# Attention and gated MLP on one core: key loads by another queue, values earlier, and the last convolutions in PSUM

## The chip, the cores and the metric

The kernel runs on one core of a Trainium2 chip. The metric is device time in microseconds; the median of the runs counts. The engines are TensorE (PE in the profile), VectorE (DVE), ScalarE (ACT), GpSimd (POOL) and SyncE (SP), which issues DMAs here. Each works through its own queue of instructions in program order; semaphores tie the queues together. The 16 DMA engines are shared by every queue that issues DMAs.

## What is computed

Four batches of 12288 queries of width 128 attend to 768 keys, which come from pooling a 384 x 32 map by 4 x 4 and a projection; the keys are also the values. The result goes through a gated projection with a causal convolution of five taps per channel.

```python
kv_pool = kv.reshape(B, H // r, r, W // r, r, C).mean(axis=(2, 4))
k = v = kv_pool.reshape(B, -1, C) @ w_sr
s = (q @ k.transpose(0, 2, 1)) / sqrt(C)
a = exp(s - s.max(-1)); a /= a.sum(-1) + 1e-9
x = a @ v
gate = sigmoid(sum(conv_w[t] * x[n + t - 4] for t in range(5)))
out = (gate * (x @ w_val)) @ w_out
```

Arrays arrive with channels first, so that the channel is the partition; the weights of the gated part arrive as 64-bit floats in one array `w_moe` and are converted on the chip.

## The kernel before

**Tiling.** A batch is 24 groups of 512 queries, a group four tiles of 128. There are 96 groups and 384 tiles in one pipeline; the order of every engine's work is written out by hand (`manual_schedule`). `t` counts tiles, `gi` and `mj` are the group and tile (0 to 3) one tile behind, and `k` is the group's place in its batch (0 to 23).

**One tile.** TensorE computes scores (`score`, L314) in three passes over a high and a low part of queries and keys, into one of three pairs of PSUM banks `s`. DVE takes the row maximum (L320), ScalarE the Exp with its sum (L325), DVE the reciprocal (L332, L334), ScalarE the high half-precision part of the probabilities (`p_hi`, L343) and DVE the low part (`p_lo`, L347). After two tiles, SyncE issues one transpose by DMA of both parts (L352) into `pt`.

**One group.** Two groups later TensorE multiplies `pt` with the values (`av_slice`, L361), in 18 products spread over four tiles; the last six need the last third of the values, high and low (`vh`, `vl`). ScalarE writes the result to `x` (L376). Convolution (GpSimd, `conv_step`, L390 and L395), tanh (L439), the two products (L443, L453), DVE's product (`g_h`, L448), eviction (L463) and store (L467) follow over the next five groups. Queries are loaded for two groups at once, in even groups (L281), and stored in even groups too.

**Preparing the next batch.** While a batch runs, the keys of the next one are made. `load_kv` (L114) loads two of 16 pieces (768 KB) into one of three buffers `kvt`, issued by SyncE in the second tile of groups 0, 1, 3, 6, 8, 10, 13 and 15. DVE sums a third of a piece per slot (`pool_kv`, L119); slots are the first three tiles of each group, counted as `3 * k + j`, and `BLOCK`, `THIRDS` and `slots` say which slot sums what: 14 slots for a quarter of the keys, of which 12 sum, one holds `column_max` (L169) and one `keys_low` (GpSimd, L212 and L214). TensorE projects a quarter at groups 7, 12, 16 and 21 (L201), ScalarE writes `vt` (L202) and the high keys (L206). A scale per column (L190 to L194, a diagonal by GpSimd at L182) follows in group 22. The values are then made in thirds: products with the diagonal (L221), a copy by ScalarE (L223), the high part (`values_high`, L226) and the low part (`values_low`, L229) on GpSimd. The first third is made in group 23, the others in groups 0 and 1 of the batch itself; the low parts come in the third tile of groups 0, 1 and 2.

**Start.** The first batch's 16 pieces are loaded by SyncE (L494), with the first queries, `w_sr`, the second half of the first query pair (`load_second`), `w_moe` and the second query pair. GpSimd adds rows of pieces 3, 6, 9 and 12 in advance (`presum`, L130), DVE sums the rest (L119), then the keys are projected and split (L142 to L155), and the pipeline begins. `trickle` holds small work that is done one item a tile, among it the conversion of `w_moe` and five diagonal matrices `dw` for a convolution on TensorE (`conv_pe`) that nothing calls.

**End.** Behind the loop stand the last seven groups, n7 to n1, from L633. GpSimd convolves n3 (`conv_pool`, L429 and L433), DVE n4, n2 and n1 (`conv_dve`, L419 and L421), n1 in two halves, with an accumulator `fast` in SBUF. `two()` takes a pair of PSUM banks, `misc()` a single one.

Of the kernel before, what the change touches and what calls it, by code (L numbers as in the profile page):

```python
# [27 lines left out]
def attn_moe_kernel(ctx, tc, qT, kvT, w_sr, w_moe, outT):  # L28
# [37 lines left out]
    dw = const.tile([C, TAPS, C], F32, name="dw")  # L66
    wval, wout, cwt = wm[:, 0:C], wm[:, C:2 * C], wm[:, 2 * C:]

    def load_moe():

        if w_moe.dtype == F32:
            nc.sync.dma_start(out=wm, in_=w_moe)
            return []
        raw, rest, more = (work.tile([C, 2 * GQ], F32, name=n, bufs=k)
                           for n, k in (("acc", 2), ("tap0", 1), ("tap1", 1)))
        raw = raw.bitcast(I32)[:, :2 * NW]
        nc.sync.dma_start(out=raw, in_=w_moe.bitcast(I32))
        words = raw.rearrange("c (n w) -> c w n", w=2)
        lo, hi = words[:, 0], words[:, 1]
        sign, ex, a = (rest.bitcast(I32)[:, i * NW:(i + 1) * NW] for i in range(3))  # L80
        t, low = more.bitcast(I32)[:, :NW], more[:, NW:2 * NW]
        v = nc.vector

        def two(out, in_, s1, op0, s2, op1, v=nc.vector):
# [25 lines left out]

    def load_kv(b, st, i):

        t = kvp.tile([C, 2, R, PC * R], F32, name="kvt")
        nc.sync.dma_start(out=t, in_=kvT[b, i:i + 2].rearrange("n c r x -> c n r x"))  # L114
# [120 lines left out]
    BLOCK = 14  # L235
    THIRDS = [n for n in range(BLOCK) if n not in (4, 9)]
    slots = {}
    for n in range(3 * PIECES):
        q, i = divmod(n, 12)
        slots[6 + BLOCK * q + THIRDS[i]] = n  # L240
    loads = {}
    for n in range(0, 3 * PIECES, 6):
        first = next(s for s, i in slots.items() if i == n) // 3
        loads.setdefault(max(first - 3, 0), []).append(n // 3)

    def setup_product(k, st):
        for q, at_k in enumerate((7, 12, 16, 21)):
            if k == at_k:
                return project_quarter(st, q)
        if k == 23:  # L250
            return values(st, 0)

    def setup_vector(k, j, st):
# [5 lines left out]
        q, n = divmod(s - 6, BLOCK)  # L259
        if n == 4 and 1 <= q <= 3:  # L260
            column_max(st, q - 1)
        if n == 9 and 1 <= q <= 3:
            keys_low(st, q - 1)
        if (k, j) == (21, 2):
            column_max(st, 3)
            st["scale"] = column_scale(st)
        if k == 22 and j < 2:
            for _ in range(3 - j):
                st["scale"].pop(0)()
        if (k, j) == (22, 2):  # L270
            keys_low(st, 3)
            st["scale"].pop(0)()

    def load_pair(g, n, parts=1):
# [4 lines left out]
        def load(i, k):  # L279
            t0 = g.t0 + i * GQ  # L280
            nc.sync.dma_start(out=q[:, i:i + k],  # L281
# [6 lines left out]
        return lambda: load(1, 1)  # L288
# [122 lines left out]
    def conv_pe(g, m, c0, c1):  # L411
        for k in range(TAPS):
            nc.tensor.matmul(m, dw[:, k], g.x[:, k + c0:k + c1], start=(k == 0),
                             stop=(k == TAPS - 1))
        return m

    def conv_dve(g, c0=0, c1=GQ):
        s = work.tile([C, GQ], F32, name="fast")[:, :c1 - c0]
        nc.vector.tensor_scalar_mul(out=s, in0=g.x[:, c0:c1], scalar1=cwt[:, 0:1])  # L419
        for k in range(1, TAPS):  # L420
            nc.vector.scalar_tensor_tensor(out=s, in0=g.x[:, k + c0:k + c1],  # L421
                                           scalar=cwt[:, k:k + 1], in1=s,
                                           op0=ALU.mult, op1=ALU.add)
        return s
# [77 lines left out]
    load_second()  # L502
    convert = load_moe()
    load_pair(at(2), at(3))
    warm = misc()
    for i in (3, 6, 9, 12):
        presum(st, i)
    k0 = c0 = 0
    low = None
    for i in range(PIECES):  # L510
# [23 lines left out]
    score(at(0), 0, early=True)  # L534
    g_qh(at(1))
# [3 lines left out]
    trickle += [lambda k=k: nc.gpsimd.tensor_scalar(  # L539
        out=dw[:, k], in0=ident, scalar1=cwt[:, k:k + 1], scalar2=1.0, op0=ALU.mult, op1=ALU.mult)  # L540
        for k in range(TAPS)]
# [6 lines left out]
    for t in range(NT * G + LAG):  # L548
# [34 lines left out]
        if gi > 1 and k < 2 and mj == 1:  # L583
            evac = values(now, k + 1)
# [18 lines left out]
        if ahead is not None and mj == 1 and k in (8, 13, 17, 22):  # L603
            keys_high(ahead, (8, 13, 17, 22).index(k))
# [4 lines left out]
        if gi >= NG and k < 3 and mj == 2:  # L609
            values_low(now, k)  # L610
# [11 lines left out]
        if mj == 3 and k == 23 and ahead is not None:  # L622
            values_high(ahead, 0)
        if mj == 3 and gi > 1 and k < 2:
            values_high(now, k + 1)
# [22 lines left out]
    gate4 = conv_dve(n4)  # L648
# [3 lines left out]
    b0, b1 = two()  # L652
    n6.m, n5.m = g_out(n6.h, b0), g_out(n5.h, b1)
    new_x(n2)
    g_x(n2, n2.av)
    avs = [c[:, :half] for c in two()]
    new_x(n1)
    for av, c in zip(avs, (0, half)):
        j = c // P
        av_range(n1, av, 0, len(AV_ORDER), j, j + NT // 2)  # L660
        if c == 0:
# [4 lines left out]
            n4.th = g_tanh(gate4)  # L666
        g_x(n1, av, c, c + half)
    a0, a1 = two()
    n4.m, n3.m = g_val(n4, a0), g_val(n3, a1)
    halo(n2, n4, nc.vector)  # L670
    gate2 = conv_dve(n2)
    n3.th = g_tanh(gate3, work.tile([C, GQ], F32, name="th2"))
    n4.h = g_h(n4.th, n4.m)
    n3.h = g_h(n3.th, n3.m, "hh")
    b0, b1 = two()
    n2.m = g_val(n2, b0)
    n4.m = g_out(n4.h, misc())
    n3.m = g_out(n3.h, b1)
    n2.th = g_tanh(gate2)
# [4 lines left out]
    n1.th = work.tile([C, GQ], F32, name="th2")  # L684
    c0, c1 = two()
    ms = [g_val(n1, m[:, :half], c, c + half) for m, c in ((c0, 0), (c1, half))]
    gates = [conv_dve(n1, 0, half)]
    n2.h = g_h(n2.th, n2.m)
    gates.append(conv_dve(n1, half, GQ))
    for gate, c in zip(gates, (0, half)):  # L690
        g_tanh(gate, n1.th[:, c:c + half])
    out_tile(n2)
    n2.m = g_out(n2.h, misc())
    hs = [g_h(n1.th[:, c:c + half], m) for m, c in zip(ms, (0, half))]
    g_evac(n2, n2.m)
    store(n2)
    outs = two()
    for h, c, o in zip(hs, (0, half), outs):
        g_evac(n1, g_out(h, o[:, :half]), c, c + half)
# [29 lines left out]
```

## Time and profile before

| what | us |
|---|---|
| runs, lowest, median and highest | 1024.54, 1026.29, 1028.73 |
| the profiled execution | 1028.8 |
| its span, first to last instruction | 1027.0 |
| mean granted TensorE clock | 0.987 |

The profile shows one execution. Its span is shorter than its time by what lies around the instructions. Times in the profile are microseconds from the start of the span, unless marked ns. A row of a timeline gives start, duration, engine, line of the kernel, operation, output and inputs by their names in the program, shapes, a count, and in brackets how long the engine idled before and who ended that. `SPq` is SyncE issuing. In rows of groups, the numbers after the bar are busy time in all, mean duration in ns, and idle time before with what ended it.

### The profile page before, as it was taken

The numbers are of one execution on the slowest core, as the hardware profiler recorded it, in microseconds if no ns is written. First come the engines' busy times: TensorE is split into PE (matmuls) and PEld (weight loads), VectorE is DVE, ScalarE is ACT, GpSimd is POOL, SyncE is SP. The second block draws the span as 40 slices with busy tenths as digits, with TensorE's granted clock in tenths as the row PEclk, the third lists the DMA queues.
The fourth block names the chain that finished last, engine by engine and source line by source line (L and its number), as shares of the span: only waits on it lengthen the run. The fifth ranks groups of instructions, "written<-read, shape, count | busy, mean of one in ns | idle before, by whom it ended". The sixth has DMA issues, their size and how long they took to land.

```text
span 1027.0 us, 15084 instructions
## 1 busy us (share of the span) xinstructions
PE 979.7 (95%) x4549; PEld 653.6 (64%) x4549; DVE 941.1 (92%) x1864; ACT 912.8 (89%) x1584; POOL 859.5 (84%) x641
## 2 busy tenths in 40 slices
PE   3789999999999999999999998999999999999997
PEld 2656666666666656666666665666666666666663
DVE  5899999999989989999999997999998999999987
ACT  1779999999989989999999997999999999999993
POOL 3349988988997978889898987898899889989983
PEclk9899999999999999999999998999999999999998
DMA  8699999999999999999999999999999999999993
GB/s 319 126 238 220 231 230 221 247 216 218 222 248 234 233 220 231 248 231 222 226 233 238 229 247 208 219 250 214 238 209 232 210 210 209 223 211 210 210 181 111
DMA packets 619329, 227.82 MB, mean 222 GB/s; under 512 B 598129, under 2 KB 598513, under 8 KB 619249
## 3 DMA queue, kind: packets, MB, share of 16 engines
q1 hardware_dynamic: 619248, 226.86, 107.3%
q8 instruction: 37, 0.61, 0.2%
q14 instruction: 44, 0.35, 0.1%
HBM read 50.66 MB, written 25.17 MB: 74 GB/s over the span
## 4 chain that ended last, share of the span: by engine, by line
PE 81%; DVE 6%; DMA 4%; POOL 3%; ACT 2%; issue 1%; POOLq 0%; DVEq 0%; ACTq 0%
PE s L314 33%; PE av L361 32%; PE m L443 7%; PE m L453 7%; DMA pt<-hl 4%; DVE hl L347 2%; DVE nm L320 2%; POOL acc L395 1%; POOL tap L390 1%; ACT hl L343 1%; ACT s L325 1%; DVE pool L119 0%; DVE h L448 0%; PE s L453 0%; PE m L221 0%
## 5 line engine op out<-in xcount | busy, mean ns | idle before, releaser
L395 POOL TENSOR_TENSOR acc<-acc,tap 128x1024 f32<-128x1024 f32 x184 | 437.0, 2375 | 6.7
L361 PE MATMUL av<-pt,vh 128*128 128x512 f16 x1140 | 408.7, 383 | 12.9 <-DMA pt<-hl 6.7
L347 DVE SCALAR_TENSOR_TENSOR hl<-s,r,hl 128x768 f16<-128x768 f32 x384 | 388.7, 1012 | 20.3 <-ACT hl L343 16.1
L320 DVE TENSOR_REDUCE nm<-s 128x1 f32<-128x768 f32 x384 | 363.1, 945 | 27.7 <-PE s L314 24.6
L343 ACT ACTIVATE hl<-s,r 128x768 f16<-128x768 f32 x384 | 346.1, 901 | 46.8 <-DVE r L334 30.4
L325 ACT ACTIVATE s<-s,nm 128x768 f32<-128x768 f32 x384 | 335.5, 874 | 23.7 <-DVE nm L320 20.6
L314 PE MATMUL s<-kh,qh 128*128 128x384 f32 x768 | 289.3, 458 | 6.8 <-DVE z L332 5.8
L361 PEld LDWEIGHTS <-vh 128*128 128x128 f16 x1164 | 113.5, 98 | 170.1 <-issue 80.9
L361 PE MATMUL av<-pt,vl 128*128 128x512 f16 x570 | 217.1, 381 | 4.5 <-POOL vl L229 4.5
L314 PEld LDWEIGHTS s<-kh,qh 128*128 128x128 f32 x768 | 146.6, 193 | 95.2 <-issue 50.2
L390 POOL TENSOR_SCALAR tap<-x,wm 128x1024 f32<-128x1024 f32 x184 | 204.1, 1123 | 0.0
L314 PE MATMUL s<-kh,ql 128*128 128x384 f32 x768 | 197.9, 338 | 0.0
L314 PE MATMUL s<-kl,qh 128*128 128x384 f32 x768 | 197.6, 338 | 0.0
L296 POOL TENSOR_TENSOR ql<-q,qh 128x512 fp32r<-128x512 f32 x96 | 122.7, 1279 | 49.5 <-ACT qh L292 49.5
L314 PEld LDWEIGHTS s<-kl,qh 128*128 128x128 f32 x768 | 140.7, 190 | 0.0
L314 PEld LDWEIGHTS s<-kh,ql 128*128 128x128 f32 x768 | 140.5, 190 | 0.0
L361 PEld LDWEIGHTS <-vl 128*128 128x128 f16 x582 | 57.6, 99 | 59.2 <-issue 32.3
L390 POOL TENSOR_SCALAR acc<-x,wm 128x1024 f32<-128x1024 f32 x46 | 51.5, 1119 | 52.3 <-ACT x L376 52.2
L453 PE MATMUL m<-h,wm 128*128 128x512 f32 x184 | 94.0, 592 | 0.7 <-DVE h L448 0.7
L443 PE MATMUL m<-x,wm 128*128 128x512 f32 x180 | 91.9, 592 | 0.0
L334 DVE RECIPROCAL r<-z 128x1 f32<-128x1 f32 x384 | 63.0, 164 | 13.1
L325 ACT ACTIVATION_READ_ACCUMULATOR s<-s,nm 128x1 f32 x384 | 74.5, 194 | 0.0
(73 smaller groups left out, 669.3 us busy)
## 6 DMA issues: line engine op xcount, KB each, us to landing
q<-in_q SPq DMA_DIRECT2D x47, 512.0 KB, 4.6
out<-o SPq DMA_DIRECT2D x47, 512.0 KB, 3.8
kvt<-in_kv SPq DMA_DIRECT2D x24, 768.0 KB, 5.5
pt<-in_kv SPq DMA_DIRECT2D x6, 768.0 KB, 9.7
pt<-hl SPq DMA_TRANSPOSE x192, 6.5
pt<-in_kv SPq DMA_DIRECT2D x4, 384.0 KB, 7.8
q<-in_q SPq DMA_DIRECT2D x2, 256.0 KB, 11.2
acc<-in_w_moe SPq DMA_DIRECT2D x1, 261.0 KB, 10.0
```

Of the source, the lines that this page charges most:

```text
L296: nc.gpsimd.tensor_tensor(out=g.ql, in0=g.q, in1=g.qh.bitcast(F32), op=ALU.subtract)
L314: nc.tensor.matmul(s[:, h, :HALF], a[:, sl], k[:, h * HALF:(h + 1) * HALF], start=(i == 0), stop=(i == 2))
L320: nc.vector.tensor_reduce(out=nm, in_=g.s[j], axis=AX.XY, op=ALU.max, negate=True)
L325: nc.scalar.activation(out=g.s[j], in_=g.s[j], func=AF.Exp, bias=g.nm.pop(j), accum_out=g.z[j])
L334: nc.vector.reciprocal(out=g.r[j], in_=z)
L343: nc.scalar.activation(out=part(g, j, 0), in_=g.s[j], func=AF.Copy, scale=g.r[j])
L347: nc.vector.scalar_tensor_tensor(out=part(g, j, 1), in0=g.s.pop(j), scalar=g.r.pop(j), in1=part(g, j, 0), op0=ALU.mult, op1=ALU.subtract)
L361: nc.tensor.matmul(out, g.st[v][:, k * P:(k + 1) * P], g.pt[:, j0:j1, a * NCH + k], start=(i == 0), stop=(i == len(AV_ORDER) - 1))
L390: nc.gpsimd.tensor_scalar(out=t, in0=g.two[:, k:k + 2 * GQ], scalar1=cwt[:, k:k + 1], scalar2=1.0, op0=ALU.mult, op1=ALU.mult)
L395: nc.gpsimd.tensor_tensor(out=g.acc, in0=g.acc, in1=t, op=ALU.add)
L443: nc.tensor.matmul(m, wval, g.x[:, HALO + c0:HALO + c1], start=True, stop=True)
L453: nc.tensor.matmul(m, wout, h, start=True, stop=True)
```

## The change

- Key loads are issued by ScalarE's queue, at the end of the second tile's work of groups 1, 3, ... 15.
- Blocks have 13 slots and begin at slot 9 instead of 6; the low keys leave the slots for the fourth tile of groups 8, 13, 17 and 21. The last projection moves from group 21 to 20, high keys from 22 to 21, the scale from 22 to 21.
- Values are made in groups 22 and 23 of the batch before and in group 0; high and low part both follow in the fourth tile of the same group.
- At the start, the second half of the first query pair, `w_moe` and the second query pair are issued by ScalarE's queue and later; pieces 6 and 10 are presummed instead of 3, 6, 9 and 12.
- `dw`, its five products and `conv_pe` are gone.
- At the end, DVE's convolutions accumulate in PSUM (`two()` for n4 and n2, `misc()` for n1), and their order changes; the banks of the values' products are used again for the outputs.

```diff
-    dw = const.tile([C, TAPS, C], F32, name="dw")
...
-        nc.sync.dma_start(out=raw, in_=w_moe.bitcast(I32))
+        nc.scalar.dma_start(out=raw, in_=w_moe.bitcast(I32))
...
     def load_kv(b, st, i):
 
         t = kvp.tile([C, 2, R, PC * R], F32, name="kvt")
-        nc.sync.dma_start(out=t, in_=kvT[b, i:i + 2].rearrange("n c r x -> c n r x"))
+        nc.scalar.dma_start(out=t, in_=kvT[b, i:i + 2].rearrange("n c r x -> c n r x"))
...
-    BLOCK = 14
-    THIRDS = [n for n in range(BLOCK) if n not in (4, 9)]
+    BLOCK, SUMS = 13, 9
+    THIRDS = [n for n in range(BLOCK) if n != 4]
     slots = {}
     for n in range(3 * PIECES):
         q, i = divmod(n, 12)
-        slots[6 + BLOCK * q + THIRDS[i]] = n
-    loads = {}
-    for n in range(0, 3 * PIECES, 6):
-        first = next(s for s, i in slots.items() if i == n) // 3
-        loads.setdefault(max(first - 3, 0), []).append(n // 3)
+        slots[SUMS + BLOCK * q + THIRDS[i]] = n
 
     def setup_product(k, st):
-        for q, at_k in enumerate((7, 12, 16, 21)):
+        for q, at_k in enumerate((7, 12, 16, 20)):
             if k == at_k:
                 return project_quarter(st, q)
-        if k == 23:
-            return values(st, 0)
+        if k in (22, 23):
+            return values(st, k - 22)
...
-        q, n = divmod(s - 6, BLOCK)
+        q, n = divmod(s - SUMS, BLOCK)
         if n == 4 and 1 <= q <= 3:
             column_max(st, q - 1)
-        if n == 9 and 1 <= q <= 3:
-            keys_low(st, q - 1)
-        if (k, j) == (21, 2):
+        if (k, j) == (20, 2):
             column_max(st, 3)
             st["scale"] = column_scale(st)
-        if k == 22 and j < 2:
-            for _ in range(3 - j):
+        if k == 21:
+            for _ in range((3, 2, 1)[j]):
                 st["scale"].pop(0)()
-        if (k, j) == (22, 2):
-            keys_low(st, 3)
-            st["scale"].pop(0)()
...
         load(0, 1)
-        return lambda: load(1, 1)
+        return lambda: load(1, 1, nc.scalar)
...
-    def conv_dve(g, c0=0, c1=GQ):
-        s = work.tile([C, GQ], F32, name="fast")[:, :c1 - c0]
-        nc.vector.tensor_scalar_mul(out=s, in0=g.x[:, c0:c1], scalar1=cwt[:, 0:1])
+    def conv_dve(g, acc, c0=0, c1=GQ):
+        nc.vector.tensor_scalar_mul(out=acc, in0=g.x[:, c0:c1], scalar1=cwt[:, 0:1])
         for k in range(1, TAPS):
-            nc.vector.scalar_tensor_tensor(out=s, in0=g.x[:, k + c0:k + c1],
-                                           scalar=cwt[:, k:k + 1], in1=s,
+            nc.vector.scalar_tensor_tensor(out=acc, in0=g.x[:, k + c0:k + c1],
+                                           scalar=cwt[:, k:k + 1], in1=acc,
                                            op0=ALU.mult, op1=ALU.add)
-        return s
...
-    load_second()
-    convert = load_moe()
-    load_pair(at(2), at(3))
     warm = misc()
-    for i in (3, 6, 9, 12):
+    for i in (6, 10):
         presum(st, i)
...
+        if i == 13:
+            load_second()
...
     score(at(0), 0, early=True)
+    convert = load_moe()
+    load_pair(at(2), at(3), eng=nc.scalar)
...
-        if gi > 1 and k < 2 and mj == 1:
-            evac = values(now, k + 1)
+        if gi > 1 and k == 0 and mj == 1:
+            evac = values(now, 2)
...
-        if ahead is not None and mj == 1 and k in (8, 13, 17, 22):
-            keys_high(ahead, (8, 13, 17, 22).index(k))
+        if ahead is not None and mj == 1 and k in (8, 13, 17, 21):
+            keys_high(ahead, (8, 13, 17, 21).index(k))
...
-        if gi >= NG and k < 3 and mj == 2:
-            values_low(now, k)
...
-        if ahead is not None and mj == 1:
-            for i in loads.get(k, ()):
-                load_kv(b + 1, ahead, i)
+        if ahead is not None and mj == 1 and k % 2 and k < PIECES:
+            load_kv(b + 1, ahead, k - 1)
...
-        if mj == 3 and k == 23 and ahead is not None:
-            values_high(ahead, 0)
-        if mj == 3 and gi > 1 and k < 2:
-            values_high(now, k + 1)
+        if ahead is not None and mj == 3 and k in (8, 13, 17, 21):
+            keys_low(ahead, (8, 13, 17, 21).index(k))
+        if mj == 3 and (k in (22, 23) and ahead is not None or k == 0 and gi > 0):
+            for f in (values_high, values_low):
+                f(ahead if k else now, (k - 22) % NG)
...
-    gate4 = conv_dve(n4)
+    acc4, acc2 = two()
+    conv_dve(n4, acc4)
...
-    b0, b1 = two()
-    n6.m, n5.m = g_out(n6.h, b0), g_out(n5.h, b1)
+    n6.m, n5.m = g_out(n6.h, a0), g_out(n5.h, a1)
     new_x(n2)
     g_x(n2, n2.av)
+    halo(n2, n4, nc.vector)
+    conv_dve(n2, acc2)
...
+    acc1 = misc()
+    conv_dve(n1, acc1[:, :half], 0, half)
     a0, a1 = two()
     n4.m, n3.m = g_val(n4, a0), g_val(n3, a1)
-    halo(n2, n4, nc.vector)
-    gate2 = conv_dve(n2)
     n3.th = g_tanh(gate3, work.tile([C, GQ], F32, name="th2"))
     n4.h = g_h(n4.th, n4.m)
     n3.h = g_h(n3.th, n3.m, "hh")
+    conv_dve(n1, acc1[:, half:], half, GQ)
+    n2.th = g_tanh(acc2)
     b0, b1 = two()
     n2.m = g_val(n2, b0)
-    n4.m = g_out(n4.h, misc())
-    n3.m = g_out(n3.h, b1)
-    n2.th = g_tanh(gate2)
+    n4.m = g_out(n4.h, a0)
+    n3.m = g_out(n3.h, a1)
+    n1.th = work.tile([C, GQ], F32, name="th2")
+    g_tanh(acc1[:, :half], n1.th[:, :half])
+    g_tanh(acc1[:, half:], n1.th[:, half:])
+    n2.h = g_h(n2.th, n2.m)
...
-    gates = [conv_dve(n1, 0, half)]
-    n2.h = g_h(n2.th, n2.m)
-    gates.append(conv_dve(n1, half, GQ))
-    for gate, c in zip(gates, (0, half)):
-        g_tanh(gate, n1.th[:, c:c + half])
+    hs = [g_h(n1.th[:, c:c + half], m) for m, c in zip(ms, (0, half))]
     out_tile(n2)
-    n2.m = g_out(n2.h, misc())
-    hs = [g_h(n1.th[:, c:c + half], m) for m, c in zip(ms, (0, half))]
+    n2.m = g_out(n2.h, b1)
...
-    outs = two()
-    for h, c, o in zip(hs, (0, half), outs):
-        g_evac(n1, g_out(h, o[:, :half]), c, c + half)
+    for h, c, o in zip(hs, (0, half), (c0, c1)):
+        g_evac(n1, g_out(h, o[:, half:]), c, c + half)
         store(n1, c, c + half)
```

More of the change, by code (lines that the diff above doesn't have):

```diff
@@ L71, in load_moe @@
         if w_moe.dtype == F32:
-            nc.sync.dma_start(out=wm, in_=w_moe)
+            nc.scalar.dma_start(out=wm, in_=w_moe)
             return []
@@ L258, in setup_vector, with load_pair, load @@
             pool_kv(st, i, a * PC // 3, (a + 1) * PC // 3)
-        q, n = divmod(s - 6, BLOCK)
+        q, n = divmod(s - SUMS, BLOCK)
         if n == 4 and 1 <= q <= 3:
             column_max(st, q - 1)
-        if n == 9 and 1 <= q <= 3:
-            keys_low(st, q - 1)
-        if (k, j) == (21, 2):
+        if (k, j) == (20, 2):
             column_max(st, 3)
             st["scale"] = column_scale(st)
-        if k == 22 and j < 2:
-            for _ in range(3 - j):
+        if k == 21:
+            for _ in range((3, 2, 1)[j]):
                 st["scale"].pop(0)()
-        if (k, j) == (22, 2):
-            keys_low(st, 3)
-            st["scale"].pop(0)()
-    def load_pair(g, n, parts=1):
+    def load_pair(g, n, parts=1, eng=nc.sync):
         q = io.tile([C, 2, GQ], F32, name="q", bufs=3)
         g.q, n.q = q[:, 0], q[:, 1]
-        def load(i, k):
+        def load(i, k, eng=eng):
             t0 = g.t0 + i * GQ
-            nc.sync.dma_start(out=q[:, i:i + k],
+            eng.dma_start(out=q[:, i:i + k],
                               in_=qT[g.b, :, t0:t0 + k * GQ].rearrange("c (i x) -> c i x", i=k))
@@ L409, in conv_step @@
             g.gate, at(g.i + 1).gate = g.acc[:, :GQ], g.acc[:, GQ:]
[L411 to L415, printed above, removed]
-    def conv_dve(g, c0=0, c1=GQ):
-        s = work.tile([C, GQ], F32, name="fast")[:, :c1 - c0]
-        nc.vector.tensor_scalar_mul(out=s, in0=g.x[:, c0:c1], scalar1=cwt[:, 0:1])
+    def conv_dve(g, acc, c0=0, c1=GQ):
+        nc.vector.tensor_scalar_mul(out=acc, in0=g.x[:, c0:c1], scalar1=cwt[:, 0:1])
         for k in range(1, TAPS):
-            nc.vector.scalar_tensor_tensor(out=s, in0=g.x[:, k + c0:k + c1],
-                                           scalar=cwt[:, k:k + 1], in1=s,
+            nc.vector.scalar_tensor_tensor(out=acc, in0=g.x[:, k + c0:k + c1],
+                                           scalar=cwt[:, k:k + 1], in1=acc,
                                            op0=ALU.mult, op1=ALU.add)
-        return s
     def conv_pool(g):
@@ L538, in attn_moe_kernel @@
     trickle += [lambda n=n: scaling[n]() for n in range(6)] + convert
-    trickle += [lambda k=k: nc.gpsimd.tensor_scalar(
-        out=dw[:, k], in0=ident, scalar1=cwt[:, k:k + 1], scalar2=1.0, op0=ALU.mult, op1=ALU.mult)
-        for k in range(TAPS)]
     def drip():
@@ L665, in attn_moe_kernel @@
             store_pair(n5)
-            n4.th = g_tanh(gate4)
         g_x(n1, av, c, c + half)
+        if c == 0:
+            n4.th = g_tanh(acc4)
+    acc1 = misc()
+    conv_dve(n1, acc1[:, :half], 0, half)
     a0, a1 = two()
     n4.m, n3.m = g_val(n4, a0), g_val(n3, a1)
-    halo(n2, n4, nc.vector)
-    gate2 = conv_dve(n2)
     n3.th = g_tanh(gate3, work.tile([C, GQ], F32, name="th2"))
@@ L683, in attn_moe_kernel @@
     store_pair(n3)
-    n1.th = work.tile([C, GQ], F32, name="th2")
     c0, c1 = two()
     ms = [g_val(n1, m[:, :half], c, c + half) for m, c in ((c0, 0), (c1, half))]
-    gates = [conv_dve(n1, 0, half)]
-    n2.h = g_h(n2.th, n2.m)
-    gates.append(conv_dve(n1, half, GQ))
-    for gate, c in zip(gates, (0, half)):
-        g_tanh(gate, n1.th[:, c:c + half])
+    hs = [g_h(n1.th[:, c:c + half], m) for m, c in zip(ms, (0, half))]
     out_tile(n2)
-    n2.m = g_out(n2.h, misc())
-    hs = [g_h(n1.th[:, c:c + half], m) for m, c in zip(ms, (0, half))]
+    n2.m = g_out(n2.h, b1)
     g_evac(n2, n2.m)
     store(n2)
-    outs = two()
-    for h, c, o in zip(hs, (0, half), outs):
-        g_evac(n1, g_out(h, o[:, :half]), c, c + half)
+    for h, c, o in zip(hs, (0, half), (c0, c1)):
+        g_evac(n1, g_out(h, o[:, half:]), c, c + half)
         store(n1, c, c + half)
```

## The prediction

> **What bounds the kernel now.** I read the page's busy shares first, then the list of the chain that ended last, then windows of one batch each, and last SyncE's own timeline.
>
> ```profile
> PE 979.7 (95%) x4549; PEld 653.6 (64%) x4549; DVE 941.1 (92%) x1864; ACT 912.8 (89%) x1584; POOL 859.5 (84%) x641
> PE 81%; DVE 6%; DMA 4%; POOL 3%; ACT 2%; issue 1%; POOLq 0%; DVEq 0%; ACTq 0%
> 936.30 1.31 PE av L361 x6
> 946.13 1.31 PE av L361 x6
> 28.60:266.70 238.10, 225.27 (x1056) 152.22 (x1055) 228.01 (x476) 217.69 (x379) 190.76 (x149) 0.99 1.08 220
> 266.70:513.50 246.80, 241.07 (x1127) 160.79 (x1125) 230.49 (x466) 227.87 (x395) 217.59 (x160) 0.99 1.12 231
> 513.50:760.10 246.60, 241.91 (x1127) 161.33 (x1125) 230.44 (x466) 227.63 (x396) 217.55 (x160) 0.99 1.13 230
> 760.10:988.80 228.70, 227.20 (x1069) 151.68 (x1067) 208.56 (x392) 215.91 (x371) 204.76 (x145) 1.00 1.08 210
> ```
>
> The two AV rows of the chain are the same place of two neighbouring groups of the last batch: a group takes 946.13 - 936.30 = 9.83 us while TensorE never waits. The four window rows begin and end at a batch's first Exp (columns: length, busy of PE, PEld, DVE, ACT, POOL, then granted clock, DMA share, GB/s); the last covers 23 groups. At 9.83 us, 24 groups are 236.0 us. Batches 0 to 2 also prepare the next batch's keys, and TensorE's part of that is small:
>
> ```profile
> L201 PE MATMUL m<-pool,wsr 128*128 128x192 f32 x8 | 2.0, 326 | 0.0
> L221 PE MATMUL m<-diag,vt 128*128 128x128 f32 x12 | 1.9, 279 | 0.0
> ```
>
> 236.0 + 2.0 + 1.9 = 239.9 us is thus what TensorE asks of batch 1 (rows of that batch). Batch 1 is 246.8 and batch 2 is 246.6, so 6.9 + 6.7 = 13.6 us are lost in them. Where, the chain and two window rows say:
>
> ```profile
> 345.61 8.11 DMA pt<-hl
> 365.93 10.10 DMA pt<-hl
> 611.20 11.36 DMA pt<-hl
> 618.40:628.60 10.20, 7.00 (x20) 3.80 (x19) 5.39 (x13) 5.16 (x9) 7.97 (x5) 0.67 1.09 212
> 201.10:211.20 10.10, 9.61 (x45) 6.25 (x43) 9.89 (x22) 9.65 (x19) 7.58 (x6) 1.00 1.12 258
> PE av L361 <- DMA pt<-hl: 6.7, 4, 3.2
> PE av L361 <- POOL vl L229: 4.5, 3, 1.5
> 299.69 0.67 POOL L229 TENSOR_TENSOR vl<-v,vh 128x256 f16<-128x256 f32 x1
> ```
>
> TensorE waits in the AV for two things: a transpose of the probabilities that lands late (four times, and a long stop also lowers the granted clock, 0.67 at 618 us), and GpSimd's low part of the last third of the values, 1.5 us once per batch from batch 1 on. SyncE's timeline tells why the transposes are late:
>
> ```profile
> 604.78 0.54 SPq L281 DMA_DIRECT2D q<-in_q  x1
> 605.42 4.55 SPq L352 DMA_TRANSPOSE pt<-hl  x1
> 610.02 0.57 SPq L114 DMA_DIRECT2D kvt<-in_kv  x1
> 610.69 0.42 SPq L467 DMA_DIRECT2D out<-o  x1
> 611.20 8.67 SPq L352 DMA_TRANSPOSE pt<-hl  x1
> 627.74 0.54 SPq L281 DMA_DIRECT2D q<-in_q  x1
> 803.11 3.64 SPq L352 DMA_TRANSPOSE pt<-hl  x1
> L352 SPq DMA_TRANSPOSE pt<-hl x192: 3556/4547/8674, 34.7 to 999.8; - x192
> L114 SPq DMA_DIRECT2D kvt<-in_kv x24: 564/575/777, 38.4 to 685.8; - x24
> ```
>
> From one q load to the next, two groups later, SyncE needs 627.74 - 604.78 = 22.96 us here, against 2 x 9.83 = 19.66 us of TensorE. A transpose with nothing ahead takes 3.64 us to issue; the one behind a key load and a store takes 8.67. With eight key loads per batch the queue falls behind until TensorE stops. In batch 3, with no key loads, TensorE is idle for 228.7 - 227.2 = 1.5 us in all, which is the values' wait: no stop on a transpose is left. So the bound is TensorE, with SyncE's queue as second bound wherever keys are loaded.
>
> **The change part by part.**
>
> *Key loads* (24, in odd groups, ScalarE's queue). SyncE loses per load the issue of 0.575 us plus about 0.1 between instructions, 8 x 0.67 = 5.4 us per batch. The load's bytes still use the 16 DMA engines, so part of the stretch of the transposes remains; but now they stand beside transposes only, in groups with no q load or store. Per pair of groups SyncE then needs, by its median, 4 x 4.547 + 0.54 + 0.42 and six gaps of 0.1, some 19.7 us: about TensorE's pace of 19.66 to 20.0 with setup, instead of 22.96. Falling behind by a fraction of a microsecond per pair, eight times, it does not reach the limit. Of the 13.6 us I leave 0.4 per batch lost: -12.8, which includes the values' wait of 1.5 in each of the two batches. Bounds: -3.0 (only that wait goes) and -13.6; somewhat lower still if L201 and L221 overlap other matmuls.
>
> What ScalarE pays is not in this trace, since it issues no DMA. Its rows:
>
> ```profile
> L343 ACT ACTIVATE hl<-s,r 128x768 f16<-128x768 f32 x384 | 346.1, 901 | 46.8 <-DVE r L334 30.4
> 404.70 0.61 ACT L292 CAST qh<-q 128x512 fp32r<-128x512 f32 x1
> 405.30 0.90 ACT L343 ACTIVATE hl<-s,r 128x768 f16<-128x768 f32 x1
> ```
>
> The load comes behind the probabilities' high part (L343, 0.90 us). ScalarE's instructions begin before the one ahead has ended (405.30 against 404.70 + 0.61), so its sequencer works ahead, and an issue of 0.575 us fits under 0.90: I cost it at nothing. Without that cover it is 24 x 0.575 = 13.8 us at most, since the next Exp queues behind it, and DVE's z, reciprocal and low part behind that. Its wait for a free key buffer is over by then: the load of group 7 takes the buffer of group 1's load, last summed in group 5. Bounds per load 0 and 0.575 by SyncE's rows, if the issue meets no other queue (a rival below).
>
> *Values a group sooner*. TensorE's and GpSimd's instructions stay in number; the last low part moves from group 2 to group 0, two groups ahead of its use. GpSimd does it where no tap runs (fourth tile), so the 1.5 us goes: -1.5 in batch 3. *Denser sums*: 13 of 13 slots hold DVE work instead of 13 of 14, 0.2 of a 0.41 us sum per group. DVE's 230.5 of 246.8 us has room; if it hasn't, 18 groups x 0.08 = 1.5 us per batch. Taken at nothing. *Keys' low parts* (four per batch on GpSimd) move to the same fourth tile, ahead of ql, which TensorE uses three tiles later: nothing. The five unused diagonal products on GpSimd (batch 0) go; nothing waits for them. *Batch 0* has the 0.5 us of the row at 201.10: -0.5.
>
> *Start.*
>
> ```profile
> 16.92 2.06 DVE L119 TENSOR_REDUCE pool<-pt 128x48 f32<-128x192 f32 x3
> 20.51 2.07 DVE L119 TENSOR_REDUCE pool<-pt 128x48 f32<-128x192 f32 x3 [1.52 <-POOL pt L130]
> 13.91 0.35 DVE L119 TENSOR_REDUCE pool<-pt 128x48 f32<-128x192 f32 x1 [1.88 <-POOL pt L130]
> 23.39 0.94 DVE L119 TENSOR_REDUCE pool<-pt 128x48 f32<-128x768 f32 x1
> 28.67 0.88 ACT L325 ACTIVATE s<-s,nm 128x768 f32<-128x768 f32 x1 [2.25 <-DVE nm L320]
> ```
>
> Piece 12 is no longer presummed by GpSimd, for which DVE idles 1.52 us; DVE sums it whole, 0.94 (four rows summed, as at 23.39) instead of 0.35 (presummed, as at 13.91). Presums move from 9 to 10 and are the same there; piece 3's goes in a stretch where DVE waits for data. 1.52 - 0.60 = 0.9, plus a little as piece 15 loses company in the DMA: -1.0. ScalarE's two late loads (2 x 0.57 at most) precede an Exp that idles 2.25 us.
>
> *End.*
>
> ```profile
> L421 DVE SCALAR_TENSOR_TENSOR fast<-x,wm,fast 128x512 f32<-128x512 f32 x8 | 9.3, 1160 | 0.3
> L448 DVE SCALAR_TENSOR_TENSOR h<-th,s 128x512 f32<-128x512 f32 x3 | 2.1, 685 | 0.7 <-PE s L443 0.4 <-ACT th L439 0.3
> L421 DVE SCALAR_TENSOR_TENSOR fast<-x,wm,fast 128x256 f32<-128x256 f32 x8 | 3.9, 485 | 0.3
> L448 DVE SCALAR_TENSOR_TENSOR h<-th,s 128x256 f32<-128x256 f32 x2 | 0.8, 416 | 0.2 <-ACT th L439 0.2
> 1023.99 0.38 ACT L463 ACTIVATE o<-s 128x256 f32<-128x256 f32 x1 [1.31 <-PE s L453]
> ```
>
> A tap in SBUF takes 1.16 us beside GpSimd; an operation of the same kind with one operand in PSUM takes 0.685. Two convs of 512 end 2 to 3 us sooner each, so DVE can do the first half of the last group's conv in the stretch where it waits for TensorE's values. From there the path loses that half, 5 x 0.485 = 2.4, and in the other half 5 x (0.485 - 0.416) = 0.3: -2.7. The two last outputs and the last eviction (1023.99) only move up. Bounds: 0 (a DVE write to PSUM, which no row shows, as dear as the 1.16) and -4.8 (both halves hidden); I take the value next to L448, which already reads PSUM.
>
> Sum: -12.8 - 1.5 - 0.5 - 1.0 - 2.7 = -18.5. The profiled execution was 1028.8 us with a span of 1027.0 (1.8 outside); the span becomes 1008.5, that execution 1010.3. The median of the runs, 1026.29, is 2.5 below the profiled one, so 1007.8.
>
> **The rivals.**
>
> *A, ScalarE's issue stands behind SyncE's transposes* (slower). SyncE issues transposes for 192 x 4.547 = 873 of 1027 us. If both queues use one descriptor generator that a transpose keeps to its end, a load meets one with chance 0.85 and waits half of it, 1.9 us, plus 0.575: 1.6 beyond the cover of 0.90. 24 x 1.6 = 38 us; ScalarE's idle time, (228.7 - 215.9) / 23 = 0.56 us per group, takes back 1.1 per pair, leaving at least 12. Middle: 25 us, so 1033. It decides once ScalarE stands over 0.8 us per load net (18.5 / 24). Nothing here speaks for or against: only one queue issues. The Trainium skill (Perfetto Trace Analysis, DMA Instruction — HWDGE (DVE, Sync)) says that generator is locked for exclusive use and that a profile counts the lock wait within the issue; by that rule this rival is the outcome, and no run here shows it yet.
>
> *B, the bytes are what is late.* Moving the issue leaves 768 KB per load on the same engines; the transposes stay as late and only the values' waits go: 1007.8 + 12.8 - 3.0 = 1017.6. For it: the DMA share of 1.12 in batch 1. Against: 1.08 in batch 3 without any lateness. The Trainium skill (DMA: Bandwidth & Descriptors, Rules for kernel authors) says spreading DMAs over queues brings no bandwidth, only issue time; by that rule B is the outcome.
>
> *C, the issue has no cover on ScalarE*, 0.3 to 0.575 us each: 24 of them give 7 to 14, so 1015 to 1021.5. For it: ScalarE is 228 of 247 us busy, its chain with DVE is tight. Against: the overlap above.
>
> **How the numbers follow.** Forecast 0.58 (its own range 1002 to 1012: tail, PE overlap and DVE bounds), B 0.13, C 0.13, A 0.16. The range leaves out A and the tips: 1001 to 1022. Half a per cent, about what a measurement of this kernel can tell from no change, is 5.1 us: faster is below 1021.2, the forecast, B and nearly all of C, 0.82; A's cheap end is the same, 0.06; the rest of A is slower, 0.12.
>
> **What would show it.** Right: batches 1 and 2 at 240 to 241 us, no AV wait on a transpose over 1 us, none on vl, key-load issues near 0.6 us on ScalarE; the first Exp near 27.7; taps near 0.69 at the end. Wrong: issues of 2 us and more on ScalarE with Exp waiting behind them (A), transposes still 8 us after a load (B), or ScalarE idle for 0.5 us before the Exp that follows each load (C).

## The result, and the profile after

The changed kernel takes 1039.91 us (median of 4 runs, 1039.43 to 1049.07), the kernel before beside it 1026.36 (1024.54 to 1028.73): ratio 1.0141, 95% interval 1.0094 to 1.0187. It is slower by 1.4% in this comparison. Sixteen later runs of it, 4 on one chip and 12 on another, have medians of 1029.4 and 1036.6 and range from 1018.9 to 1051.3, while the kernel before stays within 1024.1 and 1033.6 in all comparisons. Of its 20 runs one, of 1018.9, lies in the range of the prediction. The ratios below leave out runs over 1.5% above the fastest of their kernel; as the changed kernel spreads further than that by itself, medians of all runs stand beside them.

The profiled execution took 1039.91 us, its span is 1038.1, 11.1 longer than before. The page's first row, the shares of the chain that ended last, and the windows of one batch each, cut as before at a batch's first Exp (length, busy of PE, PEld, DVE, ACT, POOL, then granted clock, DMA share, GB/s):

```profile
PE 979.0 (94%) x4549; PEld 653.0 (63%) x4549; DVE 939.5 (91%) x1864; ACT 911.6 (88%) x1584; POOL 853.8 (82%) x632
PE 69%; DVE 12%; DMA 9%; ACT 2%; issue 2%; DVEq 0%; ACTq 0%
27.99:269.77 241.78, 225.31 (x1060) 152.18 (x1058) 228.49 (x476) 218.13 (x381) 191.82 (x147) 0.99 1.08 222
269.77:520.42 250.65, 242.28 (x1127) 161.34 (x1125) 230.29 (x466) 227.55 (x396) 217.81 (x160) 0.99 1.13 226
520.42:775.25 254.83, 243.06 (x1127) 162.08 (x1125) 230.15 (x466) 227.32 (x396) 217.62 (x160) 0.97 1.15 224
775.25:1001.85 226.60, 226.60 (x1065) 151.22 (x1063) 207.94 (x391) 215.23 (x369) 203.26 (x143) 1.00 1.08 209
```

DMA's share of the chain rose from 4 to 9%. Start, batch 3 and end became shorter as forecast: the first Exp comes at 27.99 instead of 28.67, batch 3 lost its 1.5 us of idle TensorE (226.60 long, 226.60 busy; 2.1 shorter), and from the last group's first Exp to the end of the span are 1038.1 - 1001.85 = 36.25 us instead of 1027.0 - 988.86 = 38.14. The loss is in the three batches in which keys are loaded: +3.7, +3.9 and +8.2. The list of waits (total, times, longest, in us), two steps of the chain (start, length) and the records of the two DMAs that meet (line, operation, count: shortest, median and longest issue in ns; below it shortest, median and longest time from issue to landing of the loads) say of what kind it is:

```profile
PE av L351 <- DMA pt<-hl: 21.8, 8, 8.2
325.17 12.61 DMA pt<-hl
614.12 18.25 DMA pt<-hl
L342 SPq DMA_TRANSPOSE pt<-hl x192: 3528/4558/13138, 34.0 to 1012.8; - x192
L113 ACTq DMA_DIRECT2D kvt<-in_kv x24: 374/374/403, 43.8 to 686.8; - x24
DMA to landing us min/median/max: 5.0/7.6/15.7
```

TensorE still waits for transposes of the probabilities, 21.8 us instead of 6.7. Issuing doesn't hold ScalarE up: a load takes it 0.374 us. The wait on the values' low part is gone from the list. What is late is the transpose that was already in flight when ScalarE issued a load: the chain has eight transposes, of 10.1 to 18.25 us, and in each of them a load was issued 1.0 to 3.0 us after it began. The one of 614.12 us landed 18.25 us later (the load came at 616.46), and TensorE's timeline and two windows show the stop (columns as above):

```profile
632.51 0.59 PE L351 MATMUL av<-pt,vh 128*128 128x512 f16 x1 [8.25 <-DMA pt<-hl]
614.50:622.70 8.20, 8.20 (x41) 5.61 (x40) 8.09 (x18) 7.99 (x14) 8.12 (x6) 1.00 1.09 158
622.70:632.00 9.30, 1.56 (x7) 0.73 (x5) 3.41 (x8) 3.22 (x7) 8.18 (x7) 0.74 1.24 109
```

In the stop the DMA engines are busy (1.24), yet move 109 GB/s. The view of the DMA queues, cut to the stretch in which this load's packets run (619.0 to 631.6 us), shows who is there; q1 is SyncE's queue, q10 ScalarE's (packets, MB, time of the packets as a share of 16 engines):

```profile
DMA packets 2246, 1.28 MB, mean 102 GB/s; under 512 B 1990, under 2 KB 1990, under 8 KB 2246
q1 hardware_dynamic: 1974, 0.50, 94.6%
q10 hardware_dynamic: 272, 0.79, 35.2%
```

The same view where another load of the same kernel meets almost no transpose packets (560.2 to 562.4 us):

```profile
DMA packets 540, 0.85 MB, mean 385 GB/s; under 512 B 284, under 2 KB 284, under 8 KB 540
q10 hardware_dynamic: 272, 0.79, 93.0%
q1 hardware_dynamic: 268, 0.06, 13.0%
```

The same 272 packets, 0.79 MB, take 2.2 us alone and 12.6 us among the transpose's. On average a load's packet takes 93.0% x 16 x 2.2 us / 272 = 120 ns alone and 35.2% x 16 x 12.6 / 272 = 261 ns among them; a packet on SyncE's queue takes 13.0% x 16 x 2.2 us / 268 = 17 ns beside the one load and 94.6% x 16 x 12.6 / 1974 = 97 ns beside the other. These averages hide that most packets are as fast as alone: taken one by one from the trace, the median in the slow stretch is 125 ns for the load's data packets (121 alone) and 18 ns for SyncE's (18 alone). Some 15% take over 200 ns, and 36 of the load's take 0.5 to 2.1 us. It isn't that the load's bytes come on top: both transfers together move at a quarter of the rate of the load alone, and at half of the 213 GB/s of a batch without loads (e9, below). This was the theory for the experiments, *two queues*: on one queue a load stands in line behind the transpose, on another it is served between its packets, and both crawl (move far slower together than either alone). Rivals: the bytes or the odd groups do the harm whatever queue issues them; the schedule (denser sums, earlier values) does.

### The profile page after: what moved, and what is told of

It reads as the page before. It is cut to its first block, busy times and chain, and to the rows that moved or that the text cites. A ratio compares the mean times of both kernels' runs of the same rounds, so it can differ in the third digit from the quotient of the medians.

```text
span 1038.1 us, 15114 instructions
## 1 busy us (share of the span) xinstructions
PE 979.0 (94%) x4549; PEld 653.0 (63%) x4549; DVE 939.5 (91%) x1864; ACT 911.6 (88%) x1584; POOL 853.8 (82%) x632
## 4 chain that ended last, share of the span: by engine, by line
PE 69%; DVE 12%; DMA 9%; ACT 2%; issue 2%; DVEq 0%; ACTq 0%
PE s L304 28%; PE av L351 27%; DMA pt<-hl 9%; PE m L425 6%; PE m L435 5%; DVE hl L337 5%; DVE nm L310 3%; DVE h L430 1%; DVE pool L118 1%; ACT hl L333 1%; DVE r L324 1%; ACT s L315 1%; DVE z L322 0%; PE s L435 0%; PE m L200 0%
## 5 line engine op out<-in xcount | busy, mean ns | idle before, releaser
L351 PE MATMUL av<-pt,vh 128*128 128x512 f16 x1140 | 409.9, 384 | 29.0 <-DMA pt<-hl 21.8
L435 PE MATMUL m<-h,wm 128*128 128x512 f32 x180 | 91.7, 591 | 0.0
L324 DVE RECIPROCAL r<-z 128x1 f32<-128x1 f32 x384 | 62.9, 164 | 13.1
```

The costliest lines, as they stand in the source:

```text
L324: nc.vector.reciprocal(out=g.r[j], in_=z)
L351: nc.tensor.matmul(out, g.st[v][:, k * P:(k + 1) * P], g.pt[:, j0:j1, a * NCH + k], start=(i == 0), stop=(i == len(AV_ORDER) - 1))
L435: nc.tensor.matmul(m, wout, h, start=True, stop=True)
```

## The experiments

**The queue alone (e1, e2).** e1 is the changed kernel, e2 the kernel before, each with one word of `load_kv` changed.

```diff
-        nc.scalar.dma_start(out=t, in_=kvT[b, i:i + 2]...)
+        nc.sync.dma_start(out=t, in_=kvT[b, i:i + 2]...)    # e1; e2 the other way round
```

> The changed kernel with one word put back: key loads are issued by SyncE again, at the same place of the same odd groups; values, sums, start and end stay as changed. Two rings (theory): a key load on ScalarE's queue is served packet by packet beside the transpose that SyncE already has in flight, and both crawl; on one queue they are served in order. Then this kernel is 1010 to 1021 (before 1026.3, less 0.7 of the start, 1.9 of the end, 1.5 in each of batches 1 to 3 for the values, and whatever SyncE gains from loads in odd groups), no transpose lands over 12 us after its issue, and a load lands within 9 us. Bytes or place (rival): loads in odd groups, or their bytes, make transposes late whatever queue issues them: 1030 to 1040, the stops of over 3 us on a transpose stay. Schedule (rival): denser sums or earlier values cause the loss: 1035 to 1040, and the idle time before AV is put down to DVE or GpSimd.

> The kernel before with one word changed: key loads are issued by ScalarE, at their old groups 0, 1, 3, 6, 8, 10, 13, 15; nothing else. Two rings: slower than before, 1035 to 1045 (the loss of 11 plus the 4 to 6 that start, end and values gained in the changed kernel), transposes landing up to 18 us after issue beside a load. Bytes or place: 1018 to 1027, as the queue of SyncE is relieved and nothing is worse. Schedule: 1008 to 1020, the forecast's gain without its harm.

e1: 1022.2 us (1021.2 to 1026.29, 6 runs), ratio 0.9956 (0.9939 to 0.9972): faster than both kernels, and 1.2 above the range I gave. e2: 1063.04 (1056.22 to 1077.81, 4 runs), ratio 1.0325 (1.0289 to 1.0362): right in sign and well above the range. The waits of e1 and then of e2, whose profiled execution is its longest, 1077.81:

```profile
PE av L351 <- DMA pt<-hl: 9.7, 14, 1.4
```

```profile
PE av L361 <- DMA pt<-hl: 52.0, 12, 11.7
```

In e1 fourteen stops of at most 1.4 us take the place of eight of up to 8.2; it has the schedule, bytes and groups of the changed kernel, so these three don't make the loss. In e1 no transpose landed later than 9.0 us after its issue and no load later than 5.5, both as expected.

**The place alone (e3).** The kernel before, its loads in odd groups, on SyncE.

```diff
-            for i in loads.get(k, ()):
-                load_kv(b + 1, ahead, i)
+            if k % 2 and k < PIECES: load_kv(b + 1, ahead, k - 1)
```

> The kernel before with the key loads of SyncE moved to odd groups 1, 3, ... 15; nothing else. Two rings: place does no harm, 1019 to 1027, landings as before. Bytes or place: 1030 to 1040.

1027.48 us against 1027.31, ratio 0.9994 (0.998 to 1.0009). The place alone neither harms nor helps, though by half a microsecond it lies over the range.

**Both queues in one run (e4).**

```diff
-        nc.scalar.dma_start(out=t, ...)
+        (nc.sync if i % 4 else nc.scalar).dma_start(out=t, ...)
```

> The changed kernel with loads alternating: those of groups 1, 5, 9, 13 by ScalarE, those of groups 3, 7, 11, 15 by SyncE. Two rings: late transposes (over 11 us) only beside the loads of groups 1, 5, 9, 13; between the two kernels in time, 1022 to 1033. Bytes or place: transposes late at all eight groups alike, 1033 to 1040.

1037.85 us (1029.01 to 1052.98, 6 runs), ratio 1.0067 (1.003 to 1.0103); a median above the range. In its profile, of the longest of the six runs, the two longest transposes of the chain, and the load issues nearest to them in the timeline, both ScalarE's:

```profile
416.76 17.16 DMA pt<-hl
675.05 15.93 DMA pt<-hl
```

```profile
417.19 0.44 ACTq L113 DMA_DIRECT2D kvt<-in_kv  x1
675.75 0.38 ACTq L113 DMA_DIRECT2D kvt<-in_kv  x1
```

By the starts of the Exps, the groups that last over 11 us in batches 1 and 2 are 10 and 14 of the one and 6 and 14 of the other (14.7 to 21.2 us), each one group behind a load of ScalarE's (groups 5, 9, 13); behind SyncE's loads (3, 7, 11, 15) there is none. In batch 0 it is the same: groups 10 and 14, 11.4 and 18.5 us. That is within one execution, so neither chip nor chance between runs can make it.

**Size, kind of load, issuing engine (e6, e7, e8).** e6 loads one piece per issue, in groups 1 to 16 (`dma_start(out=st["kv", i], in_=kvT[b, i])`); e7 is the kernel before with `eng=nc.scalar` in `load_pair` for the last batch's queries; e8 has `nc.gpsimd.dma_start` in `load_kv`.

> The changed kernel with each key load of 768 KB cut into two of 384 KB, both on ScalarE's queue, one in each of groups 1 to 16. Two rings, cost by the bytes that lie beside a transpose: each load then harms half as long, transposes beside loads land at most some 12 us after issue instead of 18, most within their slack, 1015 to 1032. Two rings, cost per meeting: twice as many meetings, 1040 to 1060.

> The kernel before with the query loads of the last batch (512 KB, ten of them in its even groups) issued by ScalarE; nothing else. There SyncE's queue is not behind and no key is loaded. Two rings: transposes beside these loads land 10 us and more after issue (8.4 at most before in that batch), TensorE waits there although no wait stood there before, 1028 to 1045. If only key loads, or only a queue that is behind already, do harm: 1024 to 1028.

> The changed kernel with key loads issued by GpSimd instead of ScalarE. Two rings, whichever engine issues: 1030 to 1065, transposes of over 12 us to landing. Only ScalarE's queue does it: 1010 to 1025, unless GpSimd's own time for issuing shows as longer waits for its taps.

e6: 1033.09 us (1029.71 to 1033.16), ratio 1.0048 (1.0031 to 1.0065), a little over the range for bytes, under that for meetings; the latest transpose landed 13.1 us after its issue instead of 18.2, the longest stop is 4.8 us instead of 8.2. e8: 1056.96 (1027.09 to 1072.73, 4 runs, too far apart for a ratio), transposes up to 16.1 us to landing in the execution profiled, of 1048.05: GpSimd's queue does it too. e7: 1032.63 (1026.39 to 1041.59, 10 runs), ratio 1.006 (1.0031 to 1.0089): the time came as expected, the place not. The transposes of e7 within the last batch, and behind them those of the kernel before (issue in ns; landing in us):

```profile
L352 SPq DMA_TRANSPOSE pt<-hl x46: 3518/4218/5082, 766.4 to 990.6; - x46
DMA to landing us min/median/max: 5.4/6.4/8.8
```

```profile
L352 SPq DMA_TRANSPOSE pt<-hl x47: 3556/4135/5372, 759.8 to 985.4; - x47
DMA to landing us min/median/max: 5.5/6.3/8.5
```

With SyncE not behind, a load of ScalarE's did no harm there, against my expectation. A late transpose came at the first of these loads, in batch 2, where SyncE was still behind from key loads: it issued that transpose 6.1 us after DVE had finished its input, in batch 3 at most 0.3. The transpose in the chain and the load's issue:

```profile
716.78 11.39 DMA pt<-hl
```

```profile
718.60 0.39 ACTq L281 DMA_DIRECT2D q<-in_q  x1
```

The group there lasts 15.6 us. But in this profile batch 1, in which ScalarE loads nothing, is 2.7 us longer than before as well, so not all of the difference between the two profiles is these loads'. The load at 718.60 comes 1.8 us after the transpose's issue, those of batch 3 come 2.6 to 3.1 after one. So not every meeting harms, and e12 follows up whether it is this distance that decides; e7 alone doesn't tell it from SyncE's being behind.

**No loads (e9).** As e1, with only the first three of 24 loads made; batches 1 to 3 then use keys that are not theirs, with the same work for the engines.

```diff
+        if len(kept) < 3: kept.append(kvp.tile(...)); nc.sync.dma_start(out=kept[-1], ...)
+        t = kept[i // 2 % 3]
```

> As e1, but only the first three key loads are made; the others are left out and the sums read the three buffers again, so batches 1 to 3 use keys that are not theirs (the work of the engines is the same). Loads cost what is left (theory): without them SyncE keeps the pace that the forecast gave it, no stop on a transpose, batches 1 and 2 at 240 each, 1008 to 1013, so that 21 loads on SyncE cost 9 to 14 us in e1. If instead the pace of TensorE or DVE with setup is what holds batches 1 and 2 in e1: 1018 to 1023.

1007.6 us (1007.15 to 1008.77), ratio 0.9803 (0.9779 to 0.9826). Batches 1 and 2 of e9, and then of e1:

```profile
266.72:505.36 238.64, 238.64 (x1127) 160.08 (x1125) 229.71 (x466) 227.01 (x395) 217.85 (x160) 1.00 1.08 213
505.36:744.01 238.65, 238.65 (x1127) 160.12 (x1125) 229.82 (x466) 227.24 (x396) 217.85 (x160) 1.00 1.09 212
```

```profile
269.29:512.63 243.34, 239.68 (x1127) 159.78 (x1125) 230.43 (x466) 227.85 (x395) 218.15 (x160) 1.00 1.12 234
512.63:757.66 245.03, 240.00 (x1127) 159.64 (x1125) 230.72 (x466) 228.40 (x396) 218.16 (x160) 1.00 1.12 232
```

Without loads TensorE never stands still. The 21 loads cost 1022.2 - 1007.6 = 14.6 us where SyncE issues them (13.5 between the two spans). In the changed kernel, batches 0 to 2 are 241.78 + 250.65 + 254.83 = 747.3 us, in e9 744.01 - 29.52 (its first Exp) = 714.5: there they cost 32.8. Of the 16.2 in batch 2, 254.83 - 243.06 = 11.8 is idle TensorE and 243.06 - 238.65 = 4.4 is longer time for the same 1127 matmuls, in a batch whose mean granted clock is 0.97 instead of 1.00.

**Farther apart, smaller, on SyncE (e5, e10, e15).** Attempts to win back part of the 14.6. e5 and e10 issue the loads in other groups and the first of a batch in the batch before; e15 is e1 with one piece per issue.

> Key loads on SyncE as in e1, but further apart: from batch 1 on at groups 21 (of the batch before), 0, 3, 6, 9, 11, 14, 17, and 1, 3, 5, 7, 9, 11, 14, 17 in batch 0, instead of 1, 3, ... 15; all else as in e1. SyncE's pace (theory): in e1 the queue falls behind by about 1 us per pair of groups with a load and catches up without one; with 20 groups for eight loads instead of 14 it hardly reaches the limit, the stops on transposes (9.7 us in e1) fall below 4, batches 1 and 2 are 240 to 242 each: 1014 to 1018. Bytes (rival): any load near a transpose costs the same wherever it stands: as e1, 1020 to 1025.

> As e5, with the last loads earlier: groups 0, 3, 6, 8, 10, 13, 15 (and the first of each batch from batch 2 on in group 21 of the batch before), batch 0 as in e1; e5 made DVE wait 8 us for the loads of groups 14 and 17. If only that wait spoilt e5: 1015 to 1019, no wait on a key load over 1 us. If SyncE falls behind just as much with wider gaps: 1020 to 1025.

> e1 with each load cut in two of 384 KB, in the second tile of groups 1 to 16, on SyncE. e9 puts the loads at 14.6 us in e1, 0.70 each for 21. If that is SyncE's time per load (issue and gap, about 0.67): eight more issues per batch for the next make it worse, 1026 to 1036. If it is the bytes that stand ahead of a transpose on the same queue: 1014 to 1022.

e5: 1024.69 us, ratio 0.9968 (0.9956 to 0.998); the stops on transposes fell to 3.0 us, but DVE waited 8.0 us, in three waits, for key loads. e10, without that wait: 1024.81, ratio 0.9969 (0.9949 to 0.9989), stops 13.1. Both came as their rivals said, not as the theory did. So wider gaps gain nothing, and the theory of SyncE's pace as I had put it falls. e15: 1036.77, ratio 1.0081 (1.0052 to 1.011), 0.8 over the range for time per load: twice the issues for the same bytes cost 14 us more than e1, so on SyncE the number of loads weighs more than their bytes; as half of e15's stand in even groups, beside SyncE's other work, that isn't separated further.

**Plain loads on two queues (e11).** The kernel before, half of the ten first key loads by ScalarE.

```diff
+        eng = nc.scalar if i in (1, 4, 8, 12, 15) else nc.sync
+        eng.dma_start(out=quads[i // 4][:, i % 4:i % 4 + k], ...)
```

> The kernel before with five of the ten first key loads (those that begin at pieces 1, 4, 8, 12, 15) issued by ScalarE; no transpose runs there. If only a transpose and a load harm each other: the first Exp stays at 28 to 30 us, 1024 to 1029. If any two queues do: loads land later, first Exp at 32 us or more, 1030 to 1040.

1026.52 us, ratio 1.0001 (0.998 to 1.0023), and the first Exp is early:

```profile
27.80 0.88 ACT L325 ACTIVATE s<-s,nm 128x768 f32<-128x768 f32 x1 [1.05 <-DVE nm L320]
```

The other four profiles of the kernel before's start have it at 28.67 to 30.23. Two queues of plain loads don't harm each other here; in these runs the harm appears only where one of the two carries transposes.

**The phase (e12, e14), and chance (e13, e16 to e18).** e12 and e17 are the changed kernel with `mj == 2` instead of `mj == 1` ahead of `load_kv`; e14 is e6 with the same change; e13 and e16 are the changed kernel, e18 is e1.

> The changed kernel with ScalarE's key loads at the end of the third tile of the same odd groups, 2.4 us later. Phase (theory): of the loads on a second queue in the runs so far, all those during which under 150 GB/s moved were issued 0.2 to 2.4 us after a transpose (but one that began inside another's crawl), none at 2.5 us or more. With SyncE 2 to 4.5 us behind, most loads of the changed kernel come 0.3 to 3 us after a transpose's issue; 2.4 us later most come past 2.5 us: at most three slow loads, 1018 to 1034. If the phase says nothing: 1035 to 1045.

> e12 with each load cut in two of 384 KB, in the third tile of groups 1 to 16, on ScalarE. In e12 no load crawled, yet transposes beside loads landed up to 3 us late, by about the time of the load's own packets, and TensorE waited 14.5 us. If that remainder goes with the bytes that pass ahead of a transpose: waits fall to 3 to 8 us, 1012 to 1020. If it goes with the number of meetings: 1024 to 1035.

> The changed kernel itself, unchanged, beside e14 and e15 and to be held against e12: 1034 to 1050, with some loads during which under 210 GB/s moved. If it lands at 1020 to 1030 the tile of the load says nothing and e12 was chance.

e12: 1024.86 us (1018.28 to 1034.97, 10 runs), ratio 0.9965 (0.9943 to 0.9986). e14: 1033.47 (1026.3 to 1043.99), ratio 1.0041 (1.0016 to 1.0067): smaller loads don't lower what is left. e13: 1029.42, four runs of 1018.87, 1024.42, 1034.42 and 1051.31. That made it doubtful whether the first result and e12 were the kernels' or the chips', hence three kernels on one chip:

> The changed kernel once more, on one chip with e17 and e18. Its eight runs so far are 1018.9 to 1051.3, with a median of 1039.7, those of the kernel before 1024.1 to 1033.1. Two queues, harm by chance of the phase: again a spread of over 15 us, median 1030 to 1042, above e18. If the first result was that chip's: 1018 to 1026, spread below 10.

> e12 once more beside e16. If the tile of the load decides (phase): median 1020 to 1028, at least 6 below e16. If e12 was chance: a median within 5 of e16, with runs over 1040.

> e1 once more beside e16: 1020 to 1025, spread below 8, below both others or level with e17.

| 12 runs each | median | range | ratio, 95% interval |
|---|---|---|---|
| e16, the changed kernel | 1036.55 | 1024.58 to 1047.84 | 1.0036 (1.0008 to 1.0065) |
| e17, loads in the third tile | 1024.45 | 1016.91 to 1035.1 | 0.9956 (0.9932 to 0.998) |
| e18, loads on SyncE | 1022.99 | 1020.42 to 1028.48 | 0.9943 (0.9926 to 0.996) |

The waits in the profiles of e16, e17 and e18, in this order:

```profile
PE av L351 <- DMA pt<-hl: 24.0, 10, 9.2
```

```profile
PE av L351 <- DMA pt<-hl: 11.9, 9, 2.8
```

```profile
PE av L351 <- DMA pt<-hl: 10.2, 12, 1.7
```

All three medians came as *two queues* and *phase* said; e18's spread, 8.1, is just over the 8 I gave. The spread is the changed kernel's own, and one tile later, about 2.5 us, takes back 12 us by the medians and 8 by the ratios. e18 repeats e1 and beats both kernels.

## Why the prediction was wrong, step by step

**The step that failed** is that of the key loads: "part of the stretch of the transposes remains; but now they stand beside transposes only ... Falling behind by a fraction of a microsecond per pair, eight times, it does not reach the limit", and from it -12.8 in batches 1 and 2. The batches came out at 250.65 - 246.8 = +3.9 and 254.83 - 246.6 = +8.2. The sum priced what SyncE issues and took for a load on another queue that it costs a transpose no more than one in the same queue. The runs showed in its place that such a load makes the transpose in flight late: at worst, when it begins among the transpose's packets, both slow to 102 GB/s and the transpose misses its use by 8 us; in the other stops of the changed kernel it misses it by 0.5 to 4 us. That is shown by the queue alone (e1, e2), within one run (e4), by another issuer (e8), and by e16 against e18 on one chip. Why some packets take so long is not shown by any run.

**Even on SyncE the forecast's time isn't reached.** It is reached when the loads are left out: e9's 1007.6 stands beside the forecast's 1007.8. The forecast had thus, without saying so, priced the key loads at nothing. On SyncE they cost 14.6 us for 21, in stops of about a microsecond. That the two times agree to 0.2 us is luck in part: without loads batches 1 and 2 take 238.65 us where the sum has 240.3, as TensorE asks less than its 239.9; in return e9's first Exp comes at 29.52, 0.9 later than before instead of 1.0 earlier, and its end gains 1.8 instead of 2.7.

**The other steps.** Batch 0: -0.5 forecast, +3.7 measured, for the same reason. Values a group sooner: -1.5 in batch 3, 2.1 measured, the wait is gone. Start: -1.0, measured 0.7 between the two profiles; one pair can't tell, since the first Exp comes anywhere from 27.1 to 29.8 us in the other profiles with the changed start. End: -2.7, measured 1.9 between the two profiles, but the four other profiles with the end of the kernel before take 37.1 to 37.5 us there, so 0.8 to 1.9. The taps of 512 columns in PSUM took 0.756 us where I took 0.685, and those of 256 didn't become faster:

```profile
L404 DVE SCALAR_TENSOR_TENSOR s<-x,wm,s 128x512 f32<-128x512 f32 x8 | 6.0, 756 | 0.3
L404 DVE SCALAR_TENSOR_TENSOR m<-x,wm,m 128x256 f32<-128x256 f32 x8 | 3.9, 490 | 0.3
```

ScalarE's issue at nothing was right. The load at 557 us and its neighbours on ScalarE (start, length):

```profile
557.12 0.90 ACT L333 ACTIVATE hl<-s,r 128x768 f16<-128x768 f32 x1
557.13 0.37 ACTq L113 DMA_DIRECT2D kvt<-in_kv  x1
557.92 0.88 ACT L315 ACTIVATE s<-s,nm 128x768 f32<-128x768 f32 x1
```

The issue lies wholly under the high part of the probabilities, and the Exp follows without idle time. So it is with all 24 loads: ScalarE is never idle between the instruction that covers the issue and the next.

**The rivals.** A had the sign but not the mechanism: no issue of a load took over 0.403 us, though SyncE's transposes took up to 13.1 us to issue in the same stretch. The rule on the exclusive lock (the Trainium skill, Perfetto Trace Analysis, DMA Instruction — HWDGE (DVE, Sync)) doesn't show in these records between ScalarE and SyncE. C is refuted by the rows just shown: the issue has its cover. B, the bytes, comes closest: the transposes stayed late, and the 4.6 us between its 1017.6 and e1's 1022.2 is its error with SyncE issuing. But the loss of the changed kernel isn't the bytes, since e1 moves the same. The Trainium skill (DMA: Bandwidth & Descriptors, Queues, rings and completion order) says that a DMA engine takes turns between its queues packet by packet; that 1974 and 272 packets of the two queues run in the same 12.6 us agrees with taking turns, though not with turns of one of these packets each. That some of them take up to 2 us then is what neither that rule nor my sum had in it.

## What to carry to other kernels

Before a load is moved to another queue, look at what it would have in flight beside it: a transfer that stands in line costs its own time, one that is served between the packets of a DMA transpose can cost both several times theirs (here 12.6 us instead of 2.2, and 18.25 instead of a median of 6.6). If it must be there, try its place against the transpose's issue (12 us by the medians here) and not only its size; and a kernel whose time hangs on such a meeting needs many runs, since four of them said +1.4%, and four others from -0.9 to +2.3%. Where a sum takes a stretch for removed, ask whether the sum would look the same if the transfer were left out altogether; if it does, its price is missing.

## What the runs showed of the hardware that I had not expected

- A transpose and a plain load on two queues can move at 102 GB/s together, where the load alone moves at 385 and a batch without loads at 213. Three of 24 loads on GpSimd's queue did so too (e8: 96 to 131 GB/s). The slowest query load of e7 moved at 156.
- It goes with the phase. Ten profiled runs have 264 loads on ScalarE's queue behind a first transpose. Working out for each, from the trace's packets, what all queues moved between its first and its last packet, 19 stayed under 150 GB/s. All 19 are among the 116 that were issued 0.2 to 2.45 us after the start of the latest transpose's issue; of the 139 issued later there is none, of the 9 issued sooner none either. The bounds were drawn on the five runs before e12; in the five from then on it is 3 of 54 between them and none of 90 outside. The lower bound isn't firm: in e8 a load issued 0.1 us after a transpose moved at 96 GB/s. In e17 only 4 of 24 loads fall between the bounds, in e16 12.
- The profiles of the changed kernel, e13 and e16 have one such crawl each; their other stops, of 0.3 to 4.6 us, stand beside loads that moved faster, and each follows a load. So the worst meetings alone don't make the loss, and what decides within the bounds whether a load crawls stays open.
- ScalarE issues a load in 0.374 us, SyncE the same load in 0.575, GpSimd in 0.768 (medians).
